# An unused tile of 96 bytes a partition at the right edge of SBUF

## The chip, the cores and the metric

The kernel runs on one core of one Trainium2 chip. The metric is device time in microseconds (us) of one execution; the median of three executions is 883.36 us. A time is called changed here when it moves by more than 0.2%.

## What is computed

The reference is a windowed causal attention (4 x 8 heads, 576 positions, window 64, head size 64) followed by two feed-forward layers over all 2,304 tokens:

```
scores = where(0 <= i - j < 64, q k^T / 8, -1e9);  x = softmax(scores) v     # 2304 x 512
x = relu(x @ w_in1)^2 @ w_out1                                               # 512 -> 2048 -> 512
out = elu(x @ w_in2) @ w_out2                                                # 512 -> 2048 -> 512
```

Inputs and output are 32-bit floats.

## The kernel before

**Numbers.** A large product works on split operands: `split` (L99) writes a high part with ScalarE and the rest with VectorE into an F32R tile, and `mm3` (L303) makes three matmuls of each product (high x high, high x low, low x high), each with a weight load of its own. The attention products (L224, L265, L278) take plain F32 tiles; the trace shows each of the score products (L224) as two matmul records.

**Stages.** Tokens go in five blocks (`BLOCKS`, L20: 512, 256, 512, 512, 512). For each block the attention of four head pairs gives `xs`, and for 16 slices `j` of the hidden layer `m_h` (L310) makes 12 matmuls into `ph` and `m_out` (L332) makes 12 into the four banks `o`. Attention work of the next block is set between these slices. The second layer goes in three blocks of 768 tokens: `prod` (L501, matmuls at L507) makes its first product by a scheme of seven half-size products, 384 columns wide, and `out2` (matmuls in `mm3`, L306) makes the second product, 512 columns wide, into the banks `po`, `px` and `py`. The order of all this is written out by hand. DMAs are issued on SP's queue.

**Which operand is where.** SBUF tiles come from pools. A pool takes the next place at the left end of SBUF, or at the right end with `side="right"`. On the right lie, in the first layer, the pools `sc` (`g`, `gs`) and `xp` (`xs`), L68 and L69; after `one.close()` the pools `tm` (`s`, `m`, `r`, the split `g2` under tag `gs`) and `gb`. All their tiles are multiples of 512 bytes a partition, so all begin at one remainder modulo 256. On the left lie the constants, `wts` (all weights, `y`, `xo`, `ha`, `wo`), `at` (attention) and later `wrp` (`wa`, one `xo`, `ev`). The left side begins with 512 bytes of DMA scratch (the launch code) and four small constants at 32 bytes each, 640 bytes, and its large tiles but `pb` and `pt` begin at 128 modulo 256.

So the matmuls differ in the sides of their operands:

| matmul | columns | moving operand | stationary operand |
|---|---|---|---|
| `m_h`: ph<-xs,w | 512 or 256 | xs, right | w, left |
| `m_out`: o<-gs,w | 512 or 256 | gs, right | w, left |
| `prod`: px, py, po<-xo,wa | 384 | xo, left | wa, left |
| `out2`: po, px, py<-wo,g | 512 | wo, left | g, right |

In the first block alone, the attention of head pairs 2 and 3 borrows tiles on the right for its inputs (`early`, L177): `qd` a `gs` tile, `kr` and `vr` tiles of `xs`. In all other cases `qd`, `kr` and `vr` are on the left.

By the tile sizes the right pools hold 49,152 bytes a partition in either layer, and 1,184 bytes are free between the two sides when both are fullest.

Of the kernel before, what the change touches and what calls it, by code (L numbers as in the profile page):

```python
# [10 lines left out]
F32 = mybir.dt.float32  # L11
# [5 lines left out]
P = 128  # L17
# [8 lines left out]
def window_attention_then_two_mlps(  # L26
# [32 lines left out]

    def pool(stack, name, bufs, **kw):  # L60
        return stack.enter_context(tc.tile_pool(name=name, bufs=bufs, reuse_waits="tile", **kw))

    wts = pool(ctx, "wts", 1)
    ps_a = pool(ctx, "ps_a", 2, space=PSUM)
    ps_h = pool(ctx, "ps_h", 2, space=PSUM)
    ps_o = pool(ctx, "ps_o", 1, space=PSUM)
    at = pool(att, "at", 2)
# [688 lines left out]
```

## Time and profile before

| | |
|---|---|
| median of three executions (lowest to highest) | 883.36 us (882.16 to 883.59) |
| the profiled execution: its own time, its span | 882.39 us, 880.6 us |
| TensorE matmuls, busy | 859.6 us, 98% of the span, 4,800 matmuls |
| TensorE weight loads, busy | 739.1 us, 84%, 4,800 |
| VectorE busy, ScalarE busy | 536.7 us (61%), 441.1 us (50%) |
| share of the chain that ended last, by engine | PE 95%, DMA 2% |
| granted TensorE clock, mean | 0.999 of full speed |

All views are of one profiled execution. A row of the timeline is a run of like instructions, merged: the start of the first, and the time from there to the end of the last. Ends of matmuls are modelled, so the pace of a run of matmuls is read from the start of one row to the start of the next, divided by the matmuls between.

### The profile page before, as it was taken

The page shows a single profiled execution, that of the slowest core. Times are in us where ns is not written, and L with a number is a line of the kernel's source. Part 1 is how long each engine was busy: PE and PEld are TensorE (multiplying, and loading weights), DVE is VectorE, ACT ScalarE, POOL GpSimd, SP SyncE. Part 2 cuts the span into 40 slices and gives each one's busy share as a digit, 9 for nine tenths or more (in the row PEclk, how much of TensorE's full clock was granted, in tenths as well). Part 3 has the DMA queues.
Part 4 walks back from the last instruction along what each step waited for, and adds up shares of the span by engine and source line. Part 5 has one row for each costly group of instructions (what it writes and reads, how often), then busy time and mean ns, then how long its engine had stood idle before and what let it go on. Part 6 is the DMA issues. An engine that isn't in the chain of part 4 may idle for free.

```text
span 880.6 us, 13398 instructions
## 1 busy us (share of the span) xinstructions
PE 859.6 (98%) x4800; PEld 739.1 (84%) x4800; DVE 536.7 (61%) x1355; ACT 441.1 (50%) x1022; POOL 6.3 (1%) x21
## 2 busy tenths in 40 slices
PE   5899999999999999999999999999999999999997
PEld 5687889998888888888888999978999878999876
DVE  7999857657666565764743498554455473555441
ACT  6887845544444353445655466453334452444431
POOL 2000000000000000000000000000000000000000
PEclk9999999999999999999999999999999999999999
DMA  9992114554454433424641286633555530654011
GB/s 284 360 382 58 26 49 159 163 165 122 132 182 133 165 118 122 140 97 165 238 148 44 97 322 224 216 93 102 180 155 151 154 103 13 194 157 140 25 37 36
DMA packets 79554, 128.81 MB, mean 146 GB/s; under 512 B 25216, under 2 KB 36480, under 8 KB 79488
## 3 DMA queue, kind: packets, MB, share of 16 engines
q1 hardware_dynamic: 79488, 127.95, 45.3%
q8 instruction: 38, 0.62, 0.3%
q14 instruction: 28, 0.23, 0.1%
HBM read 95.42 MB, written 32.51 MB: 145 GB/s over the span
## 4 chain that ended last, share of the span: by engine, by line
PE 95%; DMA 2%; ACT 1%; DVE 1%; SPq 1%; issue 0%; DVEq 0%
PE ph L306 23%; PE o L306 23%; PE po L306 15%; PE px L507 11%; PE py L507 6%; PE px L306 4%; PE py L306 4%; PE po L507 3%; PE pa L224 3%; PE pa L278 2%; PE pa L265 2%; DMA kr<-in_k_dram 1%; DMA vr<-in_v_dram 1%; ACT pb L237 0%; SPq L187 0%; ACT pt L106 0%
## 5 line engine op out<-in xcount | busy, mean ns | idle before, releaser
L306 PE MATMUL ph<-xs,w 128*128 128x512 f32 (+1 forms) x960 | 224.3, 376 | 2.5 <-ACT xs L101 2.2
L306 PE MATMUL o<-gs,w 128*128 128x512 f32 (+1 forms) x960 | 220.5, 374 | 0.0
L306 PEld LDWEIGHTS ph<-xs,w 128*128 128x128 f32 x960 | 166.7, 188 | 37.0 <-ACT xs L101 2.8
L306 PEld LDWEIGHTS o<-gs,w 128*128 128x128 f32 x960 | 167.5, 188 | 33.9
L306 PE MATMUL po<-wo,g 128*128 128x512 f32 x576 | 152.9, 396 | 3.6 <-ACT g L101 3.6
L306 PEld LDWEIGHTS po<-wo,g 128*128 128x128 f32 x576 | 107.6, 188 | 26.2 <-ACT g L101 4.8
L507 PE MATMUL px<-xo,wa 128*128 128x384 f32 x576 | 114.3, 336 | 0.7 <-ACT s L518 0.7
L507 PEld LDWEIGHTS px<-xo,wa 128*128 128x128 f32 x576 | 102.0, 188 | 4.7 <-ACT s L518 1.5
L324 ACT ACTIVATE g<-ph 128x512 f32<-128x512 f32 (+1 forms) x80 | 43.9, 550 | 68.7 <-PE ph L306 67.9
L102 DVE TENSOR_TENSOR gs<-g,gs 128x512 fp32r<-128x512 f32 (+1 forms) x80 | 50.8, 636 | 44.1 <-ACT gs L101 43.9
L518 ACT ACTIVATE s<-px 128x384 f32<-128x384 f32 x72 | 34.9, 488 | 81.3 <-PE px L507 80.0
L101 ACT ACTIVATE gs<-g 128x512 fp32r<-128x512 f32 (+1 forms) x80 | 46.9, 588 | 40.1 <-DVE g L328 39.2
L507 PE MATMUL py<-xo,wa 128*128 128x384 f32 x288 | 58.8, 335 | 0.0
L237 ACT ACTIVATE pb<-pb,nm 128x128 f32<-128x128 f32 x144 | 55.7, 390 | 2.7 <-DVE nm L232 2.6
L132 ACT ACTIVATE py<-praw 128x512 f32<-128x512 f32 x32 | 21.5, 672 | 64.1 <-DMA praw<-in_moe_w_out_dram 35.8
L507 PEld LDWEIGHTS py<-xo,wa 128*128 128x128 f32 x288 | 50.9, 188 | 0.7
L133 DVE TENSOR_SCALAR py<-py 128x512 f32<-128x512 f32 x32 | 13.7, 427 | 57.3 <-ACT py L132 57.2
L525 ACT ACTIVATE m<-m 128x384 f32<-128x384 f32 x72 | 36.1, 518 | 24.8 <-DVE m L524 24.8
L102 DVE TENSOR_TENSOR g<-gb,g 128x384 fp32r<-128x384 f32 x48 | 26.0, 555 | 33.6 <-ACT g L101 33.5
L101 ACT ACTIVATE g<-gb 128x384 fp32r<-128x384 f32 x48 | 24.4, 521 | 39.9 <-PE py L306 39.9
L306 PE MATMUL px<-wo,g 128*128 128x512 f32 x144 | 43.7, 397 | 0.0
L306 PE MATMUL py<-wo,g 128*128 128x512 f32 x144 | 43.4, 396 | 0.0
(87 smaller groups left out, 1001.4 us busy)
## 6 DMA issues: line engine op xcount, KB each, us to landing
wa<-wd SPq DMA_DIRECT2D x112, 256.0 KB, 2.9
wd<-wa SPq DMA_DIRECT2D x56, 256.0 KB, 3.6
wraw<-in_moe_w_in_dram SPq DMA_DIRECT2D x16, 512.0 KB, 10.1
vr<-in_v_dram SPq DMA_DIRECT2D x16, 512.0 KB, 5.0
wraw<-in_moe_w_out_dram SPq DMA_DIRECT2D x16, 512.0 KB, 10.3
praw<-in_moe_w_in_dram SPq DMA_DIRECT2D x16, 512.0 KB, 3.8
yd<-py SPq DMA_DIRECT2D x32, 256.0 KB, 2.4
praw<-in_moe_w_out_dram SPq DMA_DIRECT2D x16, 512.0 KB, 3.7
```

The costliest lines, as they stand in the source:

```text
L101: nc.scalar.activation(out=hi, in_=x, func=AF.Copy)
L102: eng.tensor_tensor(out=lo, in0=x, in1=hi.bitcast(F32), op=ALU.subtract)
L132: nc.scalar.activation(out=yf, in_=upper.bitcast(F32), func=AF.Abs)
L224: nc.tensor.matmul(out=ps[:, i * P:(i + 1) * P], lhsT=qr[:, b0 + i].rearrange("p a x -> p (a x)"), rhs=kr[:, o:o + P], start=True, stop=True,)
L237: last["act"] = nc.scalar.activation(out=pb[:, c], in_=pb[:, c], func=AF.Exp, bias=nm[:, b:b + 1], scale=-1.0, accum_out=sm[:, b:b + 1],)
L265: nc.tensor.transpose(out=ps[:, i:i + P], in_=pb[:, i:i + P], identity=ident)
L278: nc.tensor.matmul(out=ps[d, b * WIN:(b + 1) * WIN], lhsT=vr[:, b % 2, b // 2, d], rhs=pt[:, d], start=True, stop=True,)
L306: nc.tensor.matmul(out=ps, lhsT=a[x], rhs=b[y], start=(first and i == 0), stop=(last and i == 2))
L324: nc.scalar.activation(out=g[:, :n], in_=ps[:, :n], func=AF.Relu)
L507: nc.tensor.matmul(out=ps[:, :NH], lhsT=w[:, wr_, c * P:(c + 1) * P], rhs=x[:, xr_, c], start=first and n == 0, stop=last and n == 3 * CH ...
L518: nc.scalar.activation(out=s, in_=ps[:, :NH], func=AF.Copy)
L525: last["act"] = nc.scalar.activation(out=m, in_=m, func=AF.Exp)
```

## The change

A pool `pad` of one buffer is opened on the right side, ahead of all other pools there, and one tile of 24 floats a partition is taken from it. Nothing writes or reads it. It stays open to the end of the kernel, so every other tile on the right begins 96 bytes lower: at 128 modulo 256 by the change's own words, and so at 128 + 96 = 224 modulo 256 before.

```diff
     def pool(stack, name, bufs, **kw):
         return stack.enter_context(tc.tile_pool(name=name, bufs=bufs, reuse_waits="tile", **kw))
+
+    pad = pool(ctx, "pad", 1, side="right")
+    pad.tile([P, 24], F32, name="pad")
 
     wts = pool(ctx, "wts", 1)
```

## Rows read from the trace of the kernel before

**Rows 1.** The page: busy times, granted clock in 40 slices, and the chain by engine.
```profile
PE 859.6 (98%) x4800; PEld 739.1 (84%) x4800; DVE 536.7 (61%) x1355; ACT 441.1 (50%) x1022; POOL 6.3 (1%) x21
...
PEclk9999999999999999999999999999999999999999
...
PE 95%; DMA 2%; ACT 1%; DVE 1%; SPq 1%; issue 0%; DVEq 0%
```

**Rows 2.** Groups by line and shape: busy us, mean ns | idle before; matmuls 512 wide.
```profile
L306 PE MATMUL ph<-xs,w 128*128 128x512 f32 x768 | 197.1, 399 | 2.5 <-ACT xs L101 2.2 <-ACT g L324 0.2
L306 PE MATMUL o<-gs,w 128*128 128x512 f32 x768 | 194.0, 397 | 0.0
...
L306 PE MATMUL po<-wo,g 128*128 128x512 f32 x576 | 152.9, 396 | 3.6 <-ACT g L101 3.6
...
L306 PE MATMUL px<-wo,g 128*128 128x512 f32 x144 | 43.7, 397 | 0.0
L306 PE MATMUL py<-wo,g 128*128 128x512 f32 x144 | 43.4, 396 | 0.0
```

**Rows 3.** Timeline of PE in the first layer, block of 512 tokens.
```profile
455.59 2.96 PE L306 MATMUL o<-gs,w 128*128 128x512 f32 x12
458.39 2.96 PE L306 MATMUL ph<-xs,w 128*128 128x512 f32 x12
461.19 1.10 PE L306 MATMUL o<-gs,w 128*128 128x512 f32 x4
```

**Rows 4.** Timeline of PE in the second layer's last `out2` stretch.
```profile
852.41 0.86 PE L306 MATMUL po<-wo,g 128*128 128x512 f32 x3
...
874.20 0.87 PE L306 MATMUL px<-wo,g 128*128 128x512 f32 x3
```

**Rows 5.** Timeline of PE in the second layer, `prod`.
```profile
627.26 2.24 PE L507 MATMUL py<-xo,wa 128*128 128x384 f32 x12
629.34 1.20 PE L507 MATMUL po<-xo,wa 128*128 128x384 f32 x6
```

**Rows 6.** Timeline of PE in the first layer, block of 256 tokens.
```profile
140.81 1.60 PE L306 MATMUL o<-gs,w 128*128 128x256 f32 x12
142.25 1.60 PE L306 MATMUL ph<-xs,w 128*128 128x256 f32 x12
```

**Rows 7.** Groups by line and shape: weight loads from left, right and left tiles.
```profile
L306 PEld LDWEIGHTS ph<-xs,w 128*128 128x128 f32 x960 | 166.7, 188 | 37.0 <-ACT xs L101 2.8 <-ACT g L324 0.7
L306 PEld LDWEIGHTS po<-wo,g 128*128 128x128 f32 x576 | 107.6, 188 | 26.2 <-ACT g L101 4.8
L507 PEld LDWEIGHTS px<-xo,wa 128*128 128x128 f32 x576 | 102.0, 188 | 4.7 <-ACT s L518 1.5
```

**Rows 8.** Groups by line and shape: the split of a 512-wide tile, right and left.
```profile
L102 DVE TENSOR_TENSOR gs<-g,gs 128x512 fp32r<-128x512 f32 x64 | 44.0, 689 | 41.3 <-ACT gs L101 41.1
L101 ACT ACTIVATE gs<-g 128x512 fp32r<-128x512 f32 x64 | 40.3, 631 | 31.1 <-DVE g L328 30.1
...
L102 DVE TENSOR_TENSOR w<-y,w 128x512 fp32r<-128x512 f32 x4 | 2.7, 686 | 0.7 <-ACT w L101 0.7
L101 ACT ACTIVATE w<-y 128x512 fp32r<-128x512 f32 x4 | 2.5, 630 | 4.4 <-DVE y L143 4.4
```

**Rows 9.** Timeline of PE: first block, head pairs 2 and 3 (right tiles).
```profile
13.12 0.46 PE L224 MATMUL po<-kr,qd 128*128 128x128 f32 x2 [1.01 <-DMA kr<-in_k_dram]
13.41 0.27 PE L265 MATMUL pa<-ident,pb 128*128 128x128 f32 x1
13.52 1.50 PE L224 MATMUL po<-kr,qd 128*128 128x128 f32 x12
...
18.48 1.13 PE L224 MATMUL po<-kr,qd 128*128 128x128 f32 x8 [0.59 <-DMA kr<-in_k_dram]
```

**Rows 10.** Timeline of PE: the same product from left tiles, for block 2.
```profile
146.57 1.95 PE L224 MATMUL pa<-kr,qd 128*128 128x128 f32 x16
```

**Rows 11.** Group by line and shape: the product of rows 10.
```profile
L224 PE MATMUL pa<-kr,qd 128*128 128x128 f32 x224 | 28.1, 275 | 0.0
```

## The prediction

> **What bounds the kernel now.** I read the page first. Matmuls fill 98% of the span, the granted clock is 9 tenths or more in all 40 slices, and 95% of the chain that ended last is PE's [rows 1]. So the time is the sum of the matmuls' paces, at the 2.4 GHz level throughout, and a change of addresses counts only if a matmul's pace hangs on them. VectorE at 61% and ScalarE at 50% have room. Next I read the shapes [rows 2]: 2 x 768 matmuls of 512 columns with a moving operand on the right, and 576 + 144 + 144 = 864 with a stationary operand on the right; their means lie within 3 ns, but matmul ends are modelled, so these means can't price an address. The timeline can, by starts.
>
> The paces are these. `m_h` and `m_out` at 512 columns (moving right, stationary left): 2.80 us for 12, 233.3 ns [rows 3]. `out2` at 512 columns (moving left, stationary right): from 852.41 to 874.20 us stand 31 rows of three, 21.79 us / 93 = 234.3 ns [rows 4]. `prod` at 384 columns (both left): 2.08 us / 12 = 173.3 ns [rows 5]. `m_out` at 256 columns (moving right): 1.44 us / 12 = 120.0 ns [rows 6]. At a column a cycle of 2.4 GHz the columns take 213.3, 213.3, 160.0 and 106.7 ns. The rest is 20.0, 21.0, 13.3 and 13.3 ns. What the kernel could win or lose by addresses lies in this rest.
>
> **The change, part by part.** The working stands against the profiled execution, 882.39 us with a span of 880.6 us (1.8 us lie around it); it is 1.0 us, 0.11%, under the median of 883.36 us that the result is compared with.
>
> *Instructions.* The pad is never written or read, so no instruction, DMA or wait is added: 0. No order is moved. The 96 bytes fit into the 1,184 free ones, and all right tiles move together, so no tile comes to lie on another that it did not lie on before, and no wait for reuse is new. Nothing hides this term; there is nothing in it.
>
> *VectorE and ScalarE.* The split of a 512-wide tile takes 689 and 631 ns with all operands on the right, 686 and 630 ns with all on the left at 128 modulo 256 [rows 8]. That is at most 3 ns of 689, 0.2 us over 64 instructions of an engine that is not the bound: 0, between 0 and -0.2 us.
>
> *Weight loads.* 188 ns from `w` (left), from `g` (right) and from `wa` (left) [rows 7]. The remainder makes no difference to the length of a load: 0.
>
> *Plain F32 matmuls.* The trace holds a test of both remainders here. Score products from right tiles: a run of 12 takes 1.50 us; less the last one's 275 ns that is 1.225 / 11 = 111.4 ns [rows 9, 11]. From left tiles: (1.95 - 0.275) / 15 = 111.7 ns [rows 10, 11]. The same within the rounding of a row (0.01 us in 1.2). These products have both operands on one side, so they rule out a cost of the remainder 224 by itself, on either operand; they don't show one operand at 224 against the other at 128 while a weight load runs beside a matmul, as in the large products. Term: 0.
>
> *The first loads.* Right tiles take DMAs only in the first block: `qd`, `kr` and `vr` of head pairs 2 and 3. PE waited for `kr` of the two, 1.01 and 0.59 us [rows 9]. If these loads went faster, at most 1.6 us would go; I bound a loss by the same 1.6 us, having no nearer row. I take 0: the loads queue among 512 KB weight loads, so their own shape sets little.
>
> The Trainium skill has a rule that bears on this (DMA: Bandwidth & Descriptors, How a descriptor splits into AXI transactions): a transaction starts at a multiple of 256 bytes, and what lies between that and a descriptor's start is fetched for nothing. Taken for these writes, an estimate by that page is 15 beats before and 12 after for a 256-byte piece of `qd`, and 71 and 68 for 2,048 bytes of `kr`; the sum would then lie somewhat below mine, within the 1.6 us. No row here shows a transaction.
>
> *The large matmuls.* They are the open term, 1,536 of `m_h` and `m_out` and 864 of `out2`, 2,400 in all [rows 2]. After the change all operands are at 128 modulo 256, as in `prod` today. Ends: from below, the rest falls to `prod`'s 13.3 ns, since 384 columns are the nearest width that runs with both operands so: 1,536 x 6.7 = 10.2 us and 864 x 7.6 = 6.6 us, -16.8 us. From above, two streams that march in step on one remainder could meet more often: no row shows it, and I bound it by the step seen between 13.3 and 20.0 ns, 2,400 x 6.7 = +16.0 us. Value taken: m's 233.3 ns stays, and `out2` lies between 0 and 1.0 ns less, -0.4 us with half of 864 x 0.95 = 0.8 us. Why near zero: the 256-wide matmuls have the moving operand at 224 and yet the same 13.3 ns of rest as `prod` with both at 128 [rows 5, 6]. A cost of the mixed remainder should show there at least in part. The rest grows between 384 and 512 columns, on rows that differ in width and in remainder at once; width alone is enough to explain it.
>
> The Trainium skill speaks to this too (TensorE: Matmul & The Clock Gate, Part 2, step 1): the weight load and the moving operand have read ports of their own, so that loading the next weights takes nothing from the running matmul. By that rule the term is 0 and neither end exists; the 1.0 ns between [rows 3] and [rows 4], equal in width and clock, is what it leaves without a cause, and for that I keep both ends.
>
> Sum: 0 + 0 + 0 + 0 + 0 - 0.4 = -0.4 us: 882.0 us for the profiled execution, 883.0 us against the median.
>
> **The rivals.**
>
> *Faster: mixed remainders are what costs 6.7 ns.* With one operand at 224 and one at 128, the next weight load and the running matmul may collide once more in a 512-wide matmul than with both at 128. For it: 20.0 ns of rest against 13.3 [rows 3, 5], and `out2`, with the sides exchanged, differs by 1.0 ns from `m_h` [rows 3, 4]. Against it: the 256-wide matmuls, which are mixed and have 13.3 ns [rows 6]. All of it gives 883.4 - 16.8 = 866.5 us; a third of it, some 878 us. It decides from 1.77 us / 2,400 = 0.74 ns a matmul.
>
> *Slower: streams in step.* With both at one remainder the moving read and the weight read pass the same places of a 256-byte stretch together, so that a mixed offset that kept them apart is lost. For it: `out2` at 234.3 ns has its moving operand at 128 already and is the slower of the two 512-wide ones; if that alone is the cause, `m_h` and `m_out` follow it, 1,536 x 0.95 = +1.5 us, 884.8 us, just under the bound; a whole step of 6.7 ns gives 899 us. Against it: `prod` runs with both at 128 and has the least rest [rows 5]. It decides from the same 0.74 ns.
>
> *The change doesn't do what it says.* A tile that nothing touches might take no place. Then nothing moves and the time is 883.4 us; it counts with no change.
>
> **How the numbers follow.** No change, 0.2% being about what a measurement of this kernel can tell: 0.46, of which 0.03 for a pad without a place; its own range is 881.6 to 885.1 us. Faster 0.34, about a third of it the whole step to 866.5 us, the rest between. Slower 0.20, of which 0.05 above 888 us. I give 883.0 us. The range goes from 866 us, the lower end worked out, to 888 us, which is a quarter of the upper one; left out are 0.05 above and as much below 866.
>
> **What would show it.** In the profile after, the starts of runs of 12 in `m_h` and `m_out` 2.80 us apart and 93 matmuls of `out2` in 21.7 to 21.8 us would bear the forecast out; 2.72 us and 21.1 us would be the faster rival, 2.81 us and more the slower. Rows of VectorE, ScalarE and weight loads should stay within 3 ns. The forecast is wrong if a 512-wide pace moves by over 0.74 ns, or if PE's waits for `kr` in the first 20 us move by more than the 1.6 us allowed.

## The result and the profile after

The changed kernel takes 871.52 us (870.47 to 872.62) against 883.14 us: ratio 0.987, interval 0.9853 to 0.9887, 11.6 us less. A second comparison, five executions of the changed kernel, gave 869.62 us against 884.31 us, ratio 0.9823 (0.979 to 0.9856). The likeliest case of the prediction, no change, did not come; the faster rival did, in the size between its two figures.

The page of the changed kernel: engines and the chain by engine. Lines of the code have moved on by three (L306 is L309).

```profile
PE 848.2 (98%) x4800; PEld 739.6 (85%) x4800; DVE 535.9 (62%) x1355; ACT 440.6 (51%) x1022; POOL 6.2 (1%) x21
...
PE 95%; ACT 2%; DVE 1%; DMA 1%; issue 0%; SPq 0%; DVEq 0%; ACTq 0%
```

The same 4,800 matmuls take 11.4 us less of PE, while the busy times of VectorE, ScalarE and the weight loads stand where they stood [rows 1]. So the gain is in the pace of matmuls. The timeline of PE in the changed kernel, first layer, block 4 (512 tokens); below it the last `out2` stretch of the second layer, whose rows of three stand for 31 from the first to the last:

```profile
443.55 2.88 PE L309 MATMUL o<-gs,w 128*128 128x512 f32 x12
...
465.31 2.88 PE L309 MATMUL o<-gs,w 128*128 128x512 f32 x12
```

```profile
841.18 0.84 PE L309 MATMUL po<-wo,g 128*128 128x512 f32 x3
...
862.26 0.84 PE L309 MATMUL px<-wo,g 128*128 128x512 f32 x3
```

From 443.55 to 465.31 us stand 96 matmuls: 226.7 ns each, where it was 233.3 [rows 3]. From 841.18 to 862.26 us stand 93: 226.7 ns, where it was 234.3 [rows 4]. These are the paces that the faster rival named, 512 columns at 2.4 GHz and a rest of 13.3 ns. At 256 and 384 columns nothing moved (timeline of PE, block 1, and `prod`):

```profile
140.06 1.60 PE L309 MATMUL o<-gs,w 128*128 128x256 f32 x12
141.50 1.60 PE L309 MATMUL ph<-xs,w 128*128 128x256 f32 x12
...
616.21 2.25 PE L510 MATMUL px<-xo,wa 128*128 128x384 f32 x12
618.29 2.24 PE L510 MATMUL py<-xo,wa 128*128 128x384 f32 x12
```

That is 1.44 / 12 = 120.0 ns and 2.08 / 12 = 173.3 ns, as in [rows 5, 6]. VectorE and ScalarE are as predicted, too (groups by line and shape, as in [rows 8]):

```profile
L105 DVE TENSOR_TENSOR gs<-g,gs 128x512 fp32r<-128x512 f32 x64 | 44.0, 689 | 36.9 <-ACT gs L104 36.6
L104 ACT ACTIVATE gs<-g 128x512 fp32r<-128x512 f32 x64 | 40.2, 630 | 35.6 <-DVE g L331 34.4
```

**Where the worked-out 16.8 us went.** The full step was not had everywhere. Averages over start-to-start times below 260 ns (that leaves out what a wait or another product interrupts), before and after:

| matmuls, 512 columns | before, ns | after, ns | matmuls x difference, us |
|---|---|---|---|
| first layer, block 0 | 233.4 | 228.5 | 384 x 4.9 = 1.9 |
| block 2 | 233.5 | 227.6 | 384 x 5.9 = 2.3 |
| block 3 | 233.5 | 227.2 | 384 x 6.3 = 2.4 |
| block 4 | 233.3 | 226.9 | 384 x 6.4 = 2.5 |
| `out2` in runs of 12 or fewer | 233.4 | 230.9 | 270 x 2.5 = 0.7 |
| `out2` in longer runs | 234.1 | 227.8 | 594 x 6.3 = 3.7 |

The sum is 13.5 us. What is short of 16.8 us is the start of each run: after another product has come between, the first nine or so matmuls average some 229 ns in the first layer and 231 ns in the second, and from there on the pace is 226.7. This is a run of nine between two of `prod`, after and before (timeline of PE in either kernel):

```profile
623.49 2.24 PE L309 MATMUL po<-wo,g 128*128 128x512 f32 x9
625.57 1.23 PE L510 MATMUL px<-xo,wa 128*128 128x384 f32 x6
```

```profile
632.46 2.26 PE L306 MATMUL po<-wo,g 128*128 128x512 f32 x9
634.56 1.22 PE L507 MATMUL px<-xo,wa 128*128 128x384 f32 x6
```

2.08 / 9 = 231.1 ns against 2.10 / 9 = 233.3: a run that ends here has had a third of the step.

The 13.5 us against the span's 11.9 us leave 1.6 us. Most of it is TensorE's clock. In the profiled execution of the changed kernel the granted clock was 0.50 of full speed, the 1.2 GHz level, from 27.2 to 30.5 us; in that of the kernel before it was 1.00 there. The page doesn't show it: in its slices of 22 us the clock reads 9 in all 40 of either kernel. (Views by window, PE alone, after and before: the window and its length, busy time and matmuls, granted clock, DMA share, GB/s.)

```profile
27.20:30.50 3.30, 3.30 (x25) 0.50 1.03 410
```

```profile
27.20:30.50 3.30, 3.25 (x43) 1.00 1.03 412
```

The same matmuls around it, after and before (timeline of PE):

```profile
26.73 0.49 PE L309 MATMUL ph<-xs,w 128*128 128x512 f32 x1 [2.17 <-ACT xs L104]
...
31.88 0.50 PE L309 MATMUL ph<-xs,w 128*128 128x512 f32 x1
```

```profile
27.03 0.49 PE L306 MATMUL ph<-xs,w 128*128 128x512 f32 x1 [2.17 <-ACT xs L101]
...
30.87 0.50 PE L306 MATMUL ph<-xs,w 128*128 128x512 f32 x1
```

5.15 us against 3.84: the slow stretch cost 1.3 us. Ahead of it PE had been idle for 2.17 us, but so it had been in the kernel before, where the clock stayed; what makes it fall in one execution and not in another, these profiles don't show. The remaining 0.3 us is within what waits differ by from run to run. The profile of `right352` (below), with the paces of the changed kernel, has no such stretch, and its span of 867.6 us is 13.0 us under the kernel before; of its four executions the two with a mean granted clock of 0.999 took 869.4 and 869.5 us, the two with 0.997 took 870.8 and 871.8. Ahead of its last microseconds such a stretch stands in ten of the fourteen profiles of this document, in nine of them within the first 35 us; times that differ by 1 to 2 us are to be read with it.

### The profile page after: what moved, and what is told of

Same layout as the page of the kernel before. It is cut to its first block, busy times and chain, and to the rows that moved or that the text cites. A ratio compares the mean times of both kernels' runs of the same rounds, so it can differ in the third digit from the quotient of the medians.

```text
span 868.7 us, 13398 instructions
## 1 busy us (share of the span) xinstructions
PE 848.2 (98%) x4800; PEld 739.6 (85%) x4800; DVE 535.9 (62%) x1355; ACT 440.6 (51%) x1022; POOL 6.2 (1%) x21
## 4 chain that ended last, share of the span: by engine, by line
PE 95%; ACT 2%; DVE 1%; DMA 1%; issue 0%; SPq 0%; DVEq 0%; ACTq 0%
PE ph L309 23%; PE o L309 22%; PE po L309 15%; PE px L510 12%; PE py L510 6%; PE px L309 4%; PE py L309 4%; PE po L510 3%; PE pa L227 3%; PE pa L281 2%; PE pa L268 2%; PE po L227 1%; DMA praw<-in_moe_w_in_dram 1%; ACT pt L109 0%; ACT pb L240 0%; DMA wraw<-in_moe_w_in_dram 0%
## 5 line engine op out<-in xcount | busy, mean ns | idle before, releaser
L309 PE MATMUL ph<-xs,w 128*128 128x512 f32 (+1 forms) x960 | 220.8, 373 | 2.7 <-ACT xs L104 2.2
L309 PE MATMUL o<-gs,w 128*128 128x512 f32 (+1 forms) x960 | 215.8, 370 | 0.0
L309 PEld LDWEIGHTS ph<-xs,w 128*128 128x128 f32 x960 | 166.9, 189 | 33.3 <-ACT xs L104 2.8
L309 PEld LDWEIGHTS o<-gs,w 128*128 128x128 f32 x960 | 167.4, 188 | 29.6 <-DVE gs L105 0.2
L309 PE MATMUL po<-wo,g 128*128 128x512 f32 x576 | 150.5, 392 | 3.6 <-ACT g L104 3.6
L309 PEld LDWEIGHTS po<-wo,g 128*128 128x128 f32 x576 | 107.2, 188 | 24.3 <-ACT g L104 4.8
L309 PE MATMUL px<-wo,g 128*128 128x512 f32 x144 | 42.7, 390 | 0.0
L309 PE MATMUL py<-wo,g 128*128 128x512 f32 x144 | 42.5, 390 | 0.0
```

Of the source, the lines that this page charges most:

```text
L309: nc.tensor.matmul(out=ps, lhsT=a[x], rhs=b[y], start=(first and i == 0), stop=(last and i == 2))
```

## The experiments

The theory from here on: what counts is the distance between the first bytes of a matmul's moving and stationary operand, modulo 256 bytes ("distance" below: moving less stationary). Before it was 96 in `m_h` and `m_out` and -96, that is 160, in `out2`; after it is 0 in all.

### The other pads: is it the place or the distance?

```diff
-    pad.tile([P, 24], F32, name="pad")
+    pad.tile([P, 8], F32, name="pad")      # right32; 32 and 56 floats in right128 and right224
```

> The pad on the right is 32 bytes a partition instead of 96: right tiles begin at 192 modulo 256, left ones stay at 128. Theory A (each operand must itself begin at a multiple of 64 bytes; 224 does not, 128 does): 192 is such a multiple, so 512-wide matmuls of m_h, m_out and out2 reach 226.7 ns in steady stretches, as with 96 bytes, about 871 us. Theory B (moving and stationary operand must have one remainder modulo 64, wherever they begin): the same, 871 us. Theory C (one remainder modulo 256 or 128 is needed): 192 against 128 is 64 off, so the paces stay at 233.3 and 234.3 ns or nearly so, 880 to 884 us.

> The pad on the right is 128 bytes: right tiles begin at 96 modulo 256, that is 32 modulo 64 as in the kernel before, left ones at 128. Theories A, B and C all leave the 512-wide paces at 233.3 and 234.3 ns, 882 to 884 us. If moving the right side by any amount is what helps (theory D, a pad as such or a shift of the tiles' far addresses), the paces fall to 226.7 ns and the time to 871 us.

> The pad on the right is 224 bytes: right tiles begin at 0 modulo 256, left ones at 128. Theories A and B: a multiple of 64 and one remainder modulo 64, 226.7 ns, 871 us. Theory C with modulo 128: the same. Theory C with modulo 256: 128 off, paces 231 to 234 ns, 880 to 884 us.

`left96` has no pad on the right and this one on the left:

```diff
+    lpad = pool(ctx, "lpad", 1)
+    lpad.tile([P, 24], F32, name="lpad")
+
     wts = pool(ctx, "wts", 1)
```

> No pad on the right; a pad of 96 bytes on the left ahead of wts instead, so that all weights, xo, wa, wo begin at 224 modulo 256, as the right tiles do in the kernel before. Theory A (own start at a multiple of 64): nothing is at such a multiple now, so the 512-wide matmuls keep 233 to 241 ns and the 384-wide ones of prod (1,008) lose up to 6.7 ns each: 883 to 890 us. Theory B or C (one remainder for both operands): 226.7 ns at 512 columns, 173.3 ns at 384, 871 us.

Measured, one time each, beside 883.57 us for the kernel before: `right32` 876.37, `right128` 881.54, `right224` 878.53, `left96` 874.07 us. Timelines of PE, first layer, block 4: `left96`, `right32`, `right128`, `right224` (84 matmuls from the first to the last row of each).

```profile
444.48 2.88 PE L309 MATMUL ph<-xs,w 128*128 128x512 f32 x12
...
463.52 2.88 PE L309 MATMUL o<-gs,w 128*128 128x512 f32 x12
```

```profile
445.28 2.91 PE L309 MATMUL o<-gs,w 128*128 128x512 f32 x12
...
464.51 2.91 PE L309 MATMUL ph<-xs,w 128*128 128x512 f32 x12
```

```profile
444.08 2.96 PE L309 MATMUL o<-gs,w 128*128 128x512 f32 x12
...
463.68 2.96 PE L309 MATMUL ph<-xs,w 128*128 128x512 f32 x12
```

```profile
444.88 2.95 PE L309 MATMUL ph<-xs,w 128*128 128x512 f32 x12
...
464.40 2.95 PE L309 MATMUL o<-gs,w 128*128 128x512 f32 x12
```

`left96` (distance 0, everything at 224): 19.04 / 84 = 226.7 ns. `right32` (64): 228.9. `right128` (224): 233.3. `right224` (128): 232.4. Theory A falls, as operands at 224 run at the full pace once both are there, and `right224`'s multiples of 64 do not. B falls, for 64 and 128 modulo 256 have the same remainder modulo 64 and neither is at 226.7. D falls with `right128`. Left is C, with modulo 256; only that the paces between lie so unevenly was in no expectation. The times that C gave for 64 and 128 bytes, 880 to 884 us, were too high, as `right32` and `right224` show. `left96` has the paces of the changed kernel in every width and yet 874 us: PE waited 2.5 us once in block 2 for VectorE's part of an `xs`, which it did not in the changed kernel's profiled run, and right behind that wait the granted clock was 0.50 from 251.9 to 255.2 us: PE took 6.35 us from the score products at 251.09 us to the second row of large matmuls behind them, and 4.52 us in the changed kernel.

### No tile moved: the weights' columns alone

```diff
-                [w[:, r, m * P:(m + 1) * P] for r in range(2)],
+                [at_byte(w, r, m, 96) for r in range(2)],      # and the same in m_h
```

`at_byte(w, r, m, b)` is the slice of the line above it, taken `b` bytes further on.

> No pad and no tile moved: the kernel before, with the stationary slices of m_h and m_out read 96 bytes (24 columns) further on, so that they begin at 224 modulo 256 like their moving operands (the slice that would run past its tile is read 416 bytes earlier instead, which is the same remainder). The first layer's products thus use shifted weight columns. Theory R (what counts is the distance between where the two operands of one matmul begin, modulo 256): m_h and m_out at 512 columns go to 226.7 ns, out2 stays at 234.3 ns, the first layer ends 7 to 8 us earlier, 875 to 876 us. Theory T (where tiles lie matters for some other reader or writer, VectorE, ScalarE or DMA): nothing changes, 883 us.

875.68 us beside 882.21 us. The timeline of PE in block 4 (84 matmuls):

```profile
444.47 2.88 PE L314 MATMUL o<-gs,w 128*128 128x512 f32 x12
...
463.51 2.88 PE L314 MATMUL ph<-xs,w 128*128 128x512 f32 x12
```

226.7 ns, with every tile and every operand of VectorE and ScalarE where it was before, and `out2` still at 234.3 ns. (In the first 194 us the order of some attention products, decoding steps and loads differs from the kernel before; from there on every matmul has its old place.) The first layer's last matmul starts 6.6 us earlier (488.31 us against 494.93). So the pad works by where the operands of the matmuls begin, relative to each other; theory T falls. Whether a matmul's own weights count or those that are loaded beside it, this run can't tell, as all weights moved alike.

### Half of it

```diff
+    pad = pool(one, "pad", 1, side="right")
+    pad.tile([P, 24], F32, name="pad")
     xp = pool(one, "xp", 2, side="right")
```

> The 96 bytes lie between the pools sc and xp: xs begins at 128 modulo 256, gs stays at 224, and the second layer's right tiles are at 224 as before. Theory R: m_h runs at 226.7 ns, m_out at 233.3 ns, in turns within one stretch, out2 at 234.3 ns; about half of the first layer's gain, 879 to 880 us. If a pace hangs on the whole stretch or on the pad as such, both run alike, at one pace or the other.

884.08 us beside 882.21 us: no gain in the time, a miss. The timeline of PE, block 4:

```profile
451.88 2.98 PE L308 MATMUL o<-gs,w 128*128 128x512 f32 x12
454.70 2.92 PE L308 MATMUL ph<-xs,w 128*128 128x512 f32 x12
457.46 2.98 PE L308 MATMUL o<-gs,w 128*128 128x512 f32 x12
460.27 2.92 PE L308 MATMUL ph<-xs,w 128*128 128x512 f32 x12
```

`m_h` at distance 0 takes 2.76 / 12 = 230.0 ns, and `m_out` at 96 takes (2.82 + 2.81) / 24 = 234.6, worse than before. Inside the twelve of `m_h` the starts are some 231 ns apart on average for the first eight and 226 to 227 for the last four: each run of `m_out` throws it back, much as `prod` does with the nine slow matmuls of `out2` behind it.

The reason why the time shows no gain lies in the first 35 us. The granted clock was at the 1.2 GHz level twice in this profile (view by window, PE alone):

```profile
19.30:22.60 3.30, 3.30 (x15) 0.50 1.04 402
29.60:32.80 3.20, 3.20 (x23) 0.50 1.03 410
```

At the row of eight score products that starts at 19.30 us here and at 18.48 before, PE was 0.8 us behind the kernel before; at the `ph` row of 34.49 us (30.87 before) it was 3.6 us behind. From there to the last `m_out` of the first layer it made up 1.9 us, where the changed kernel gains 8.6 us from the same row on. So half the operands in step are worth something, but far less than half, and in this execution the clock took more than that.

### The sweep

```diff
-                [w[:, r, c * P:(c + 1) * P] for r in range(2)],
+                [at_byte(w, r, c, byte(t, j)) for r in range(2)],
```

The line shown is that of `m_h`; `m_out` has the same one, and the pad has 88 floats.

> A pad of 352 bytes brings the right tiles to 128 modulo 512, the remainder of the left ones, and in the first layer the stationary slices are then read at a distance from their moving operand that changes every two hidden slices (so the products use shifted weight columns): 0 to 224 bytes in steps of 32 in block 1 (256 columns) and block 2, 256 to 480 in block 3, and 4, 8, 16, 24 bytes to either side of 0 in block 4. Theory R with modulo 256: block 3 repeats block 2, 226.7 ns at 0 and 256, near 229 at 64, 232 to 234 at the others. R with modulo 512: 0 and 256 differ, one of them at 226.7 ns. If only a match of the first bytes counts, the paces at 4 to 24 bytes are 233 ns; if the reads meet in places of 32 bytes or more, those stay at 226.7 ns. Time itself: 873 to 884 us, of no use here.

In block 4 each distance has 48 matmuls, four rows. The first and the third row of +8, +16 and +24 bytes, 24 matmuls from one to the other (timeline of PE):

```profile
450.08 2.96 PE L327 MATMUL ph<-xs,w 128*128 128x512 f32 x12
...
455.68 2.96 PE L327 MATMUL ph<-xs,w 128*128 128x512 f32 x12
...
461.27 2.90 PE L327 MATMUL ph<-xs,w 128*128 128x512 f32 x12
...
466.75 2.90 PE L327 MATMUL ph<-xs,w 128*128 128x512 f32 x12
...
472.23 2.94 PE L327 MATMUL ph<-xs,w 128*128 128x512 f32 x12
...
477.78 2.94 PE L327 MATMUL ph<-xs,w 128*128 128x512 f32 x12
```

+8 bytes: 5.60 / 24 = 233.3 ns; +16: 5.48 / 24 = 228.3; +24: 5.55 / 24 = 231.3. All distances, from steady stretches of starts in this trace (ns):

| distance, bytes | 512 columns | 256 columns |
|---|---|---|
| -16, -8, -4 | 233.3, 230.6, 232.3 | |
| 4, 8, 16, 24 | 233.3, 233.3, 228.3, 231.1 | |
| 32 | 233.3 | 116.7 |
| 64 | 228.9 | 117.8 |
| 96 | 233.3 | 120.0 |
| 160 | 234.3 | 117.5 |
| 192 | 233.3 | 117.8 |
| 288, 320, 352, 416, 448 | as 32, 64, 96, 160, 192 | |

At 0 and 256 a run of 512 columns settles at 226 to 227 ns after its first nine; 128, 224 and -24 have no long run here (`right224` and `right128` gave 232.4 and 233.3 for the first two). Block 3 repeats block 2 to within 0.2 ns, so the modulus is 256. The paces of this one trace give those of all the others by the distance alone: 233.3 ns at 96 and 234.3 at 160 are `m_h` and `out2` before [rows 3, 4], 228.9 at 64 is `right32`. Four bytes off 0 already cost nearly the whole step: of the two expectations for block 4, that of the first bytes is the nearer, though 16 bytes give 228.3 ns. And at 256 columns, 0 and 96 are alike and the slowest of all.

### The modulus with an ordinary pad, and the 256-column block

```diff
-    pad.tile([P, 24], F32, name="pad")
+    pad.tile([P, 88], F32, name="pad")
```

> The pad on the right is 352 = 96 + 256 bytes. Theory R with modulo 256: as with 96 bytes, 226.7 ns and 870 to 873 us. R with modulo 512: the distance is 0 instead of 256 modulo 512, a pace and a time of its own.

870.15 us (869.42 to 871.78), ratio 0.9833 (0.98 to 0.9865): the time of the changed kernel, modulo 256. In the kernel of the next experiment the block of 256 tokens reads and writes its tiles 32 bytes further on:

```diff
+    def off(t):
+        return 8 if t == 1 else 0
...
-                [g[:, r, :n] for r in range(2)],
+                [g[:, r, off(t):off(t) + n] for r in range(2)],      # and so for xs, and in both splits
```

> The changed kernel, and in the block of 256 tokens alone xs and gs are written and read 32 bytes into their tiles, so that these 384 matmuls have a distance of 32 bytes instead of 0; nothing else moves and the result is the reference's. In the sweep this distance gave 116.7 ns at 256 columns against 120.0 at 0. If that holds without the rest of the sweep: 384 x 3.3 = 1.3 us less than the changed kernel, 870 us; if PE in this block waits for attention work in between, less or nothing of it is seen, 871 to 872 us.

> The changed kernel once more, beside block1_off32 on one chip: 870 to 873 us, ratio 0.985 to 0.989.

869.42 us (868.69 to 871.84), ratio 0.9827 (0.9793 to 0.986), beside 869.62 us (868.28 to 870.71) for the changed kernel itself. The timeline of PE in block 1:

```profile
140.08 1.56 PE L313 MATMUL o<-gs,w 128*128 128x256 f32 x12
141.48 1.56 PE L313 MATMUL ph<-xs,w 128*128 128x256 f32 x12
```

1.40 / 12 = 116.7 ns: the pace came, the 1.3 us cannot be told from no gain by these times. From the first `m_out` of block 1 to that of block 2 the profiles show 64.1 us against 65.0.

### 384 columns

```diff
-                    ps[:, :NH], lhsT=w[:, wr_, c * P:(c + 1) * P], rhs=x[:, xr_, c],
+                    ps[:, :NH], lhsT=at_byte(w, wr_, c, -BYTE[b][p]), rhs=x[:, xr_, c],
```

> The changed kernel with prod's stationary slices read at a distance that changes with the hidden pair p: 0 to 224 bytes in steps of 32 in the first and third block of 768 tokens, 4 to 24 bytes to either side of 0 in the second (prod then uses shifted weight columns). Theory R holds for every width: steady runs of 384 columns leave 173.3 ns at most distances, by up to 6.7 ns upwards. Theory W (the distance only costs at 512 columns, and at 256 columns 0 is even the worst): prod stays within 172 to 175 ns everywhere, time 870 to 873 us.

872.06 us, within the range that theory W gave for the time; the paces lie between the two theories. A stretch of `prod` in its first block (timeline of PE):

```profile
522.95 1.22 PE L524 MATMUL px<-xo,wa 128*128 128x384 f32 x6
...
528.23 2.28 PE L524 MATMUL px<-xo,wa 128*128 128x384 f32 x12
```

The same 30 matmuls in the changed kernel, all at distance 0:

```profile
521.98 1.23 PE L510 MATMUL px<-xo,wa 128*128 128x384 f32 x6
...
527.21 2.25 PE L510 MATMUL px<-xo,wa 128*128 128x384 f32 x12
```

5.28 / 30 = 176.0 ns against 5.23 / 30 = 174.3 (`out2` comes right ahead, so that the start of this run is slow in either kernel). Over all `prod` matmuls behind the ninth of their run the traces give 175.4 ns against 173.4. So the distance counts at 384 columns too, by about 2 ns on average; which distance belongs to which stretch is not told apart, as PE's order mixes the pairs.

### Which load does a matmul meet?

```diff
-        s = sc.tile([P, 2, NMAX], F32R, tag="gs", name="gs", bufs=GB)
+        z = sc.tile([P, 2 * NMAX + 64], F32R, tag="gs", name="gs", bufs=GB)
+        s = [z[:, 0:NMAX], z[:, NMAX + 24:2 * NMAX + 24]]
...
+                    out=ps[:, :n], lhsT=at_byte(w, x, m, 96 if AT[t] == i else 0), rhs=g[y][:, :n],
```

> The changed kernel with the low half of gs 96 bytes further on (224 modulo 256; its tile is 256 bytes longer), so that of the three matmuls of a product in m_out the second has its moving operand at 224, the others at 128. In block 2 the stationary slice of the second matmul is read 96 bytes on too (each matmul matches its own weights); in block 3 that of the third matmul (each moving operand matches the weights that are loaded while it streams); in block 4 none. The first layer thus uses some shifted weight columns. Theory N (a running matmul meets the load of the next matmul's weights): block 3 is at 226.7 ns in m_out and m_h, blocks 2 and 4 at 230 to 234. Theory O (a matmul meets its own stationary operand): block 2 is at 226.7 ns, blocks 3 and 4 at 230 to 234. Time between 872 and 880 us under both.

874.12 us beside 882.43 us. Neither theory's 226.7 ns came in `m_out`. A run of each kind, block 2 (own weights), block 3 (next weights) and block 4 (none); timeline of PE:

```profile
298.90 2.94 PE L354 MATMUL o<-gs,w 128*128 128x512 f32 x12
301.67 2.91 PE L319 MATMUL ph<-xs,w 128*128 128x512 f32 x12
...
396.81 2.91 PE L354 MATMUL o<-gs,w 128*128 128x512 f32 x12
399.56 2.91 PE L319 MATMUL ph<-xs,w 128*128 128x512 f32 x12
...
446.54 2.94 PE L354 MATMUL o<-gs,w 128*128 128x512 f32 x12
449.32 2.92 PE L319 MATMUL ph<-xs,w 128*128 128x512 f32 x12
```

`m_out` takes 2.77, 2.75 and 2.78 us for 12: 230.8, 229.2 and 231.7 ns; over all its unbroken rows in these blocks the averages are 231.2, 229.9 and 231.3. Matching the next weights is the best of three by a little, but far from the full pace, so this run doesn't decide between the two. It does show a limit of the theory above. In block 2 every large matmul is at distance 0 from its own weights, in block 3 from the next ones, and neither has the 226.7 ns: neither distance alone is enough. Wherever 226.7 ns was measured, all moving and stationary operands of the stretch began at one remainder.

## Why the prediction was right in its range and wrong in its likeliest case

The measured 871.5 us lies in the range, on the side of the rival that had 0.34, and not in the case that had 0.46. By the sign that the prediction set itself, a pace at 512 columns that moves by over 0.74 ns, its likeliest case is wrong: the paces moved by 6.7 and 7.6 ns. That the time lies in the range is owed to the bounds, which were kept for a rival, and not to the mechanism that was expected.

*What held.* PE's pace is the time; no instruction was added and each engine kept its order; VectorE, ScalarE and the weight loads did not move. The plain F32 matmuls stayed at 111 ns, with both operands on one side before and after, distance a multiple of 256. The bounds of the large matmuls held, and the lower one gave the pace: 226.7 ns in steady stretches.

*The step that failed* is the value taken between the bounds for the large matmuls, -0.4 us where the paces measured give -13.5 us. Its reason is "Why near zero": the 256-wide matmuls were at 224 against 128 and had the same 13.3 ns of rest as `prod`, so a cost of mixed remainders "should show there at least in part". The sweep shows that it need not: at 256 columns distance 0 and 96 both give 120.0 ns, while 32 gives 116.7. I compared two widths as if one curve of distance held for both, and by chance the row stood at a distance where the 256-column pace is the one that it has at 0. The other reading, that the 1.0 ns between `m_h` and `out2` is an effect of addresses since nothing else differed, was in the text as the reason for keeping the bounds and deserved more weight: in the sweep those two paces are the values at 96 and 160.

*The size.* The rival's 16.8 us assumed the steady pace for all 2,400 matmuls. The first nine or so after each interruption run slower, at some 229 to 231 ns; that took most of the 3.3 us between 16.8 and 13.5. The stretch at the 1.2 GHz level took another 1.3 us of the profiled execution; the prediction had the 2.4 GHz level throughout.

*The slower rival* fell: operands in step are the best case at 384 and 512 columns, not the worst. Its one observation, `out2` slower than `m_h` with the moving operand already at 128, goes with the distance, 160 against 96.

*The first loads.* PE's wait for `kr` went from 1.6 us to 0.5 us in the first profile, and over all profiles with the early tiles at 128 modulo 256 it lies between nothing (`block1_off32`) and 2.0 us (`sweep`). The bound of 1.6 us held; a gain by the descriptors' alignment is not told from the spread.

The Trainium skill says that loading the next weights takes no read bandwidth from the running matmul (TensorE: Matmul & The Clock Gate, Part 2, step 1). The term of 0 that the prediction drew from it does not agree with these runs: in `shift_weights` it was the weights' start alone that moved, and a matmul took 6.7 ns less. Whether the sentence itself fails, that is, whether it is the load beside a matmul that costs the time, no run here shows.

*What stays open.* That it is the concurrent weight load which the moving read meets is argued, from the weights being what was shifted; it is not shown, since no kernel here ran without a load beside each matmul, and the last experiment didn't separate the next matmul's weights from its own; matching either alone was not enough. Why a run needs about nine matmuls to settle is open as well.

## What to carry to other kernels

Where matmuls of F32R operands with a weight load each bound a kernel, compare the start-to-start time of a steady run with the columns' time, and look where in a partition of SBUF each operand starts: at 384 and 512 columns the pace was best here with all of them at the same place modulo 256 bytes, which a tile of some bytes can arrange. At 256 columns another distance (32 bytes here) had the better pace, though the time didn't show it. Long unbroken runs of one width get the full pace; a run of nine gets a third of the step. Bringing half of the operands into step gains far less than half. And before a difference of 1 to 2 us is put down to a change, look at the granted clock of the first stretches in either profile.

## What the runs showed of the hardware that was not expected

- With one distance for all matmuls of a stretch, the pace at 512 columns hangs on that distance modulo 256: 226.7 ns at 0, 228.3 at 16, 228.9 at 64, and 230.6 to 234.3 at the others measured; 4 bytes from 0 it is already 232.3 to 233.3.
- It is not the alignment of either operand: both at 224 modulo 256 run like both at 128.
- Matching each matmul to its own weights alone, or to the next ones alone, is not enough: 231.2 and 229.9 ns (`which_load`).
- At 256 columns the order is another: 116.7 ns at 32, 120.0 at 0.
- The full pace is reached after about nine like matmuls and lost by what came between here: an attention product, a `prod`, or matmuls at another distance.
- The granted clock can fall to the 1.2 GHz level for a few us in one execution and not in another of like work: 1.3 us in the changed kernel's profile, none in that of `right352`.
